# A planned attention and MLP kernel: weight loads on a second queue, more key and query buffers, a step split in two, and a new order

## The chip, the cores and the metric

The kernel runs on one core of a Trainium2 chip. Its engines are TensorE (PE in the profile, with its weight loads as PEld), VectorE (DVE), ScalarE (ACT), GpSimd (POOL) and SyncE (SP). SP, ACT and POOL each have a queue from which they issue transfers (DMAs). The metric is the device time of one execution in microseconds (us), as the median of several runs.

## The reference

Eight batches and eight heads of head dimension 64 are computed. There are 512 local and 32 global positions in a batch. A local query attends to all 32 global keys and to the local keys within 32 positions of it; a global query attends to all 544 keys. The attention output, 4352 tokens of width 512, goes through an MLP.

```python
s_g   = scale * q_g @ concat(k_g, k_l).T;   out_g = softmax(s_g) @ concat(v_g, v_l)
s_ll  = where(|i - j| <= 32, scale * q_l @ k_l.T, -1e9)
s_lg  = scale * q_l @ k_g.T
out_l = softmax(concat(s_lg, s_ll)) @ concat(v_g, v_l)
x     = concat(out_g, out_l) as tokens x 512
out   = gelu(x @ w_in) @ w_out              # w_in 512 x 2048, w_out 2048 x 512
```

All is float32.

## The kernel before

**Units and chunks.** Attention is cut into 64 units: a batch, a half of its sequence (256 queries) and a pair of heads. Four units make one chunk, the 256 tokens of a batch's half, which then goes through the MLP; 16 such chunks and one for all global tokens ("g") make 17 passes of the MLP. A unit's steps are: its loads (lk, lq, lv), transposes of keys and queries (tk, tq), copies of these to SBUF (k1, q1), scores (s, L408, and sg for the global queries, L565), mask and maximum (m, L427), the exponential (e, on ACT), the scaling (n, then nf and ns), transposes of the attention weights (t, L482 to L485), copies of these (ah), the product with the values (o, L519 or L532), and copies to the MLP's input (x). In a chunk's MLP, h is the first product (L707, or L711 to L713), g the GELU, mo the second product (L738, or L746 to L748), ob the copy of the result and ow its store.

**Precision.** The first eight units and the first chunk's MLP use plain float32 products. Later ones use pairs of a high and a low part, three products instead of one.

**Weights.** There are 32 loads of 512 KB (wl, L152 and L156), 16 of w_in and 16 of w_out. Each is worked on by w1 (L161 on DVE or L163 on ACT), w2 (L167, ACT) and w3 (L172, DVE) before the first chunk's MLP uses it, and by w4 and w5 (high and low part) before the second chunk's does. The raw loads have 16 buffers. Load number i also waits for w1 of load i - NW, with NW = 10. All 32 loads are issued from SP's queue.

**Loads of the first eight units.** They come in pairs of units. Keys go out on SP's queue, the first two pairs' queries on ACT's and the others' on SP's, and values on POOL's queue, nine transfers for a pair. The float32 keys and queries of a unit are copied into tiles of tag k1 and q1 with the unit's parity, so that two units have a place each.

**The order.** Nothing is ordered by hand. A planner in the kernel file gives each step a cost (DUR), a due time (from formulas, and OFF by kind of step), engines that may do it (EARLY, LATER), what it needs, and which buffers it takes and frees. It then plays a list schedule, and the instructions are emitted in the order of that play; each engine runs its own in that order. For transfers the planner keeps one running time of the DMA engines.

**The scaling.** st_n (L451 to L461) adds a small constant to the sums, takes the reciprocal, and multiplies 128 x 512 weights by it, all on DVE. nf (L468) and ns (L473) then write scaled copies of the edges; t waits for ns.

**The end.** The last chunk's two results (ob, t = 0 and 1) are copied from PSUM, each by one instruction. For "g" each is stored by four transfers: for t = 0 all four on SP's queue, for t = 1 two on SP's and two on ACT's.

## Time and profile before

| what | value |
|---|---|
| time, median of 3 runs | 1037.21 us (1036.88 to 1037.89) |
| the profiled execution's own time | 1037.63 us |
| its span, first to last instruction | 1035.8 us |
| PE busy | 1011.0 us (98%) |
| PEld busy | 898.3 us (87%) |
| DVE busy | 660.2 us (64%) |
| ACT busy | 688.2 us (66%) |
| POOL busy | 400.1 us (39%) |
| mean granted TensorE clock | 0.999 |
| moved by DMA | 72.29 MB, mean 70 GB/s |

Busy time is the time in which an engine has an instruction of its own under way; waits for semaphores and the issuing of DMAs from SP and ACT are not in it. Matmuls are pipelined, and their ends are modelled. The time of an execution stands 1.8 us above its span, which is what lies around the program.

### The profile page before, as it was taken

The page shows a single profiled execution, that of the slowest core. Times are in us where ns is not written, and L with a number is a line of the kernel's source. Part 1 is how long each engine was busy: PE and PEld are TensorE (multiplying, and loading weights), DVE is VectorE, ACT ScalarE, POOL GpSimd, SP SyncE. Part 2 cuts the span into 40 slices and gives each one's busy share as a digit, 9 for nine tenths or more (in the row PEclk, how much of TensorE's full clock was granted, in tenths as well). Part 3 has the DMA queues.
Part 4 walks back from the last instruction along what each step waited for, and adds up shares of the span by engine and source line. Part 5 has one row for each costly group of instructions (what it writes and reads, how often), then busy time and mean ns, then how long its engine had stood idle before and what let it go on. Part 6 is the DMA issues. An engine that isn't in the chain of part 4 may idle for free.

```text
span 1035.8 us, 21369 instructions
## 1 busy us (share of the span) xinstructions
PE 1011.0 (98%) x7000; PEld 898.3 (87%) x7000; DVE 660.2 (64%) x2068; ACT 688.2 (66%) x1637; POOL 400.1 (39%) x462
## 2 busy tenths in 40 slices
PE   7989999999999999999999999999999999999998
PEld 4656688899998999999998999999998999999997
DVE  3889757677676857677776667676776677651000
ACT  4889865777676866776677756676777757663231
POOL 6322676424333334243343434243343434233121
PEclk9999999999999999999999999999999999999999
DMA  6995222223323223222322323222322323210000
GB/s 148 279 316 149 51 68 47 49 63 60 71 40 73 41 61 60 58 50 54 65 51 60 66 61 61 59 48 55 71 45 62 62 61 62 49 28 22 22 21 21
DMA packets 271519, 72.29 MB, mean 70 GB/s; under 512 B 255984, under 2 KB 264432, under 8 KB 271408
## 3 DMA queue, kind: packets, MB, share of 16 engines
q1 hardware_dynamic: 267920, 68.44, 28.9%
q0 software_dynamic: 1280, 1.84, 0.7%
q8 instruction: 55, 0.90, 0.4%
q10 hardware_dynamic: 2208, 0.66, 0.3%
q14 instruction: 56, 0.46, 0.2%
HBM read 61.41 MB, written 9.44 MB: 68 GB/s over the span
## 4 chain that ended last, share of the span: by engine, by line
PE 88%; DVE 4%; DMA 3%; ACT 3%; issue 1%; SPq 1%; DVEq 0%; ACTq 0%
PE h L711 12%; PE acc L746 11%; PE h L712 11%; PE h L713 11%; PE acc L748 11%; PE acc L747 11%; PE o L519 5%; PE s L408 4%; DMA wraw<-in_moe_w_in_dram 3%; PE t L482 2%; PE go L652 2%; PE sg L565 1%; PE t L483 1%; PE acc L738 1%; ACT a_t L281 1%
## 5 line engine op out<-in xcount | busy, mean ns | idle before, releaser
L141 POOL TENSOR_TENSOR gl<-gf,gh 128x512 fp32r<-128x512 f32 x127 | 166.0, 1307 | 353.7 <-ACT gh L134 257.8
L711 PE MATMUL h<-xh,wh 128*128 128x256 f32 x1024 | 294.2, 287 | 0.0
L712 PE MATMUL h<-xl,wh 128*128 128x256 f32 x1024 | 286.3, 280 | 0.5 <-DVE xl L141 0.5
L713 PE MATMUL h<-xh,wl 128*128 128x256 f32 x1024 | 285.9, 279 | 0.0
L746 PE MATMUL acc<-wh,gh 128*128 128x512 f32 x512 | 205.9, 402 | 0.0
L748 PE MATMUL acc<-wl,gh 128*128 128x512 f32 x512 | 200.7, 392 | 0.0
L747 PE MATMUL acc<-wh,gl 128*128 128x512 f32 x512 | 200.3, 391 | 0.0
L711 PEld LDWEIGHTS h<-xh,wh 128*128 128x128 f32 x1024 | 192.7, 188 | 7.7 <-ACT gf L281 0.6
L712 PEld LDWEIGHTS h<-xl,wh 128*128 128x128 f32 x1024 | 192.7, 188 | 5.9 <-DVE xl L141 0.7
L713 PEld LDWEIGHTS h<-xh,wl 128*128 128x128 f32 x1024 | 194.1, 190 | 0.0
L281 ACT ACTIVATE gf<-h 128x512 f32<-128x512 f32 x136 | 81.2, 598 | 80.9 <-PE h L713 48.9
L281 ACT ACTIVATE a_t<-a_t,sm 128x192 f32<-128x192 f32 (+1 forms) x256 | 116.6, 457 | 4.5 <-DVE sm L433 3.9
L748 PEld LDWEIGHTS acc<-wl,gh 128*128 128x128 f32 x512 | 96.1, 188 | 21.3
L141 POOL TENSOR_TENSOR vs<-vr,vs 128x512 fp32r<-128x512 f32 x56 | 73.0, 1303 | 98.2 <-ACT vs L134 39.2
L746 PEld LDWEIGHTS acc<-wh,gh 128*128 128x128 f32 x512 | 96.3, 188 | 12.8
L134 ACT ACTIVATE gh<-gf 128x512 fp32r<-128x512 f32 x106 | 67.0, 632 | 60.4 <-PE acc L748 58.2
L747 PEld LDWEIGHTS acc<-wh,gl 128*128 128x128 f32 x512 | 96.5, 188 | 11.6 <-POOL gl L141 0.3
L502 DVE TENSOR_TENSOR at<-t,at 128x512 fp32r<-128x512 f32 x112 | 68.5, 617 | 49.9 <-ACT at L134 49.3
L427 DVE CUSTOM_DVE_ANT_0 a_t<-s,mask 128x192 f32<-128x192 f32 (+1 forms) x256 | 78.9, 367 | 25.4 <-PE s L408 25.4
L281 ACT ACT_TABLE_LOAD x67 | 86.0, 1283 | 1.1
L134 ACT ACTIVATE at<-t 128x512 fp32r<-128x512 f32 x112 | 60.0, 543 | 31.8 <-PE t L483 16.1
L545 ACT ACTIVATE xs<-o 64x256 f32<-64x256 f32 x112 | 42.6, 381 | 52.3 <-PE o L519 49.5
(140 smaller groups left out, 1743.0 us busy)
## 6 DMA issues: line engine op xcount, KB each, us to landing
wraw<-in_moe_w_in_dram SPq DMA_DIRECT2D x16, 512.0 KB, 7.5
raws<-in_v_l_dram SPq DMA_DIRECT2D x64, 128.0 KB, 2.5
wraw<-in_moe_w_out_dram SPq DMA_DIRECT2D x16, 512.0 KB, 9.0
out_dram<-ob SPq DMA_DIRECT2D x32, 256.0 KB, 2.3
raws<-in_k_l_dram SPq DMA_DIRECT2D x224, 36.0 KB, 1.9
raws<-in_q_l_dram SPq DMA_DIRECT2D x224, 32.0 KB, 1.8
vr<-in_v_l_dram SPq DMA_DIRECT2D x112, 64.0 KB, 2.2
raws<-in_v_g_dram SPq DMA_DIRECT2D x128, 16.0 KB, 2.0
```

Source lines behind the costliest of these rows:

```text
L134: nc.scalar.activation(out=out, in_=in_, func=AF.Copy)
L141: (nc.vector if e == "v" else nc.gpsimd).tensor_sub(**kw)
L281: nc.scalar.activation(func=func, **kw)
L427: nc.vector.tensor_tensor_reduce(out=a_t[:, j, aoff[half][i]:aoff[half][i] + w], in0=s[:, c:c + w], in1=masks[half][i], scale=1.0, scalar= ...
L502: nc.vector.tensor_sub(out=at[:, 1], in0=st.pop((u, "t", j))[:, :n * P].rearrange("p (n q) -> p n q", q=P), in1=at.bitcast(F32)[:, 0])
L519: nc.tensor.matmul(out=o[:, :, qsl], lhsT=l.rearrange("p s e -> p (s e)"), rhs=r, start=(n == 0), stop=(n == 3), skip_group_check=True)
L711: nc.tensor.matmul(out=h, lhsT=hi, rhs=xh, start=(c == 0 and not (key == (0, 0) and f < HQ and f % 2)), stop=False, skip_group_check=True)
L712: nc.tensor.matmul(out=h, lhsT=hi, rhs=xl, start=False, stop=False, skip_group_check=True)
L713: nc.tensor.matmul(out=h, lhsT=lo, rhs=xh, start=False, stop=(c == NCC - 1), skip_group_check=True)
L746: nc.tensor.matmul(out=acc[t], lhsT=gh[:, f % 2, tsl], rhs=hi, start=(f == 0), stop=False)
L747: nc.tensor.matmul(out=acc[t], lhsT=gl[:, f % 2, tsl], rhs=hi, start=False, stop=False)
L748: nc.tensor.matmul(out=acc[t], lhsT=gh[:, f % 2, tsl], rhs=lo, start=False, stop=(f == NF - 1))
```

## The change

- A weight's load may be issued from SP's or from POOL's queue; of the 32, 24 now go out on POOL's. The load waits for w1 of the load 12 places before it, not 10. Values of the first eight units may go out on SP's queue or POOL's.
- The float32 keys and queries of the first eight units have four places instead of two (tags k1, k2 and q1, q2, each with the unit's parity).
- The big multiplication leaves st_n and becomes a step st_nm of its own. For the first eight units the planner may put it on POOL or DVE, later on DVE. nf needs n only; t needs nm and ns.
- The last result (t = 1 of "g") is copied in two halves, one by ACT and one by DVE. For t = 0 of "g" two of the four stores move from SP's queue to POOL's.
- The second pair's queries' load waits for the transposes of the first unit's keys; tq of a unit comes after its tk; the first weight's load comes after lh of batch 0 instead of lk of the first unit.
- The planner's costs, its due times (OFF, and a new table TWEAK by step) and its model of transfers change: it now counts eight transfers in flight for POOL's queue and eight for the others together. With this the order of the whole program is new.

```diff
-    "n": 1.08, "nf": {"p": 1.0, "v": 0.36}, "ns": {"p": 0.42, "v": 0.22}, "t0": 0.44, "t1": 0.33,
+    "n": 0.24, "nm": {"v": 0.8, "p": 1.25}, "nf": {"p": 0.65, "v": 0.36}, "ns": {"p": 0.42, "v": 0.22}, "t0": 0.44, "t1": 0.33,
...
-NW = 10
+NW = 12
...
-            (nc.sync if e == "s" else nc.scalar).dma_start(out=raw, in_=w_out.bitcast(I32)[f * P:(f + 1) * P, :])
+            (nc.sync if e == "s" else nc.gpsimd).dma_start(out=raw, in_=w_out.bitcast(I32)[f * P:(f + 1) * P, :])
...
-        t = ap_.tile([P, CH], F32, name="qt", tag=f"q1{u[2] % 2}")
+        t = ap_.tile([P, CH], F32, name="qt", tag=f"q{1 + second(u)}{u[2] % 2}")
...
-        t = ap_.tile([P, NB, 32], F32, name="kt", tag=f"k1{u[2] % 2}")
+        t = ap_.tile([P, NB, 32], F32, name="kt", tag=f"k{1 + second(u)}{u[2] % 2}")
...
+    def st_nm(e, u):
+        a_t = a_ts[u[2] % 2]
...
-        nc.vector.tensor_tensor(out=av, in0=av, in1=edges(u)[0].unsqueeze(3).to_broadcast([P, 2, 2, P]), op=ALU.mult)
+        (nc.vector if e == "v" else nc.gpsimd).tensor_tensor(out=av, in0=av, in1=edges(u)[0].unsqueeze(3).to_broadcast([P, 2, 2, P]), op=ALU.mult)
...
-        copy(e, o, acc)
+        if key == "g" and t:
+            copy("a", o[:, 0:CH], acc[:, 0:CH])
+            copy("v", o[:, CH:DM], acc[:, CH:DM])
+        else:
+            copy(e, o, acc)
...
-                (nc.sync if t == 0 or n % 2 == 0 else nc.scalar).dma_start(out=out[r0:r0 + SG, :], in_=o[32 * n:32 * n + 32])
+                ((nc.sync, nc.gpsimd)[n % 2] if t == 0 else (nc.sync, nc.scalar)[n % 2]).dma_start(out=out[r0:r0 + SG, :], in_=o[32 * n:32 * n + 32])
...
-        step(("wl", n), w_load, (n,), "s", due - 6.0, [("w1", wl[i - NW])] if i >= NW else [], [("wr", n)], issues=0.9, size=0.36, after=("wl", wl[i - 1]) if i else ("lk", units[0]))
+        step(("wl", n), w_load, (n,), "sp", due - 6.0, [("w1", wl[i - NW])] if i >= NW else [], [("wr", n)], issues=1, size=0.36, after=("wl", wl[i - 1]) if i else ("lh", 0))
...
-        if k in "as" and x["size"]:
-            t = max(t, dma - (1.5 if k == "a" else 2.7))
+        if x["size"] and len(lanes[k == "p"]) > 7:
+            t = max(t, lanes[k == "p"][-8] + 0.1)
```

## Rows read from the trace of the kernel before

**Rows 1.** Windows: busy time (count) by engine, granted clock, DMA share, GB/s.

```profile
4.24:25.00 20.76, 17.70 (x70) 11.52 (x70) 8.97 (x37) 9.06 (x30) 12.50 (x24) 1.00 0.70 147
25.00:110.00 85.00, 76.22 (x415) 54.76 (x415) 73.17 (x211) 74.54 (x163) 29.41 (x40) 1.00 0.78 234
110.00:200.00 90.00, 86.30 (x568) 72.03 (x567) 66.33 (x181) 66.06 (x160) 55.80 (x53) 1.00 0.26 52
200.00:1030.80 830.80, 830.42 (x5954) 759.99 (x5953) 511.74 (x1642) 536.68 (x1283) 298.76 (x330) 1.00 0.25 52
```

**Rows 2.** Waits of PE over the span: total us, times, longest.

```profile
PE sg L565 <- DMA vrb<-in_v_g_dram: 2.3, 1, 2.3
...
PE kp L321 <- ACT kt L134: 1.3, 2, 0.7
...
PE kp L321 <- ACT qt L134: 1.0, 2, 0.6
```

**Rows 3.** Timeline of ACT, first 30 us; idle before and releaser in brackets.

```profile
17.38 0.38 ACT L134 ACTIVATE qt<-qp 128x256 f32<-128x256 f32 x1 [1.67 <-PE s L408]
...
26.09 0.38 ACT L134 ACTIVATE qt<-qp 128x256 f32<-128x256 f32 x1 [0.24 <-PE s L408]
```

**Rows 4.** Timeline of PE, first 30 us.

```profile
9.00 1.86 PE L408 MATMUL s<-kt,qt 64*128 64x192 f32 x8
...
24.98 0.97 PE L408 MATMUL s<-kt,qt 64*128 64x192 f32 x8
```

**Rows 5.** Timeline of SP's queue: its first issue and its first weights' issue.

```profile
0.76 0.45 SPq L304 DMA_DIRECT2D raws<-in_k_l_dram  x1
...
23.01 1.69 SPq L152 DMA_DIRECT2D wraw<-in_moe_w_in_dram  x3
```

**Rows 6.** The raw weights' tile, to 110 us: durations in ns, first and last start.

```profile
L172 DVE SCALAR_TENSOR_TENSOR wf<-wraw x32: 673/684/1943, 31.9 to 100.1; 128x512 int32<-128x512 int32 x32
L161 DVE TENSOR_SCALAR wraw<-wraw x18: 412/428/2027, 28.9 to 95.0; 128x512 int32<-128x512 int32 x18
...
DMA to landing us min/median/max: 3.9/8.4/14.4
```

**Rows 7.** Timeline of POOL: issues of value loads at three times, and a subtraction.

```profile
5.08 1.68 POOL L253 DMA_DIRECT2D vr<-in_v_l_dram  x2
...
30.24 1.53 POOL L253 DMA_DIRECT2D vr<-in_v_l_dram  x2 [13.30 <-PE o L532]
...
57.38 0.54 POOL L264 DMA_DIRECT2D vrb<-in_v_g_dram  x1 [2.17 <-DMA vrb<-in_v_l_dram]
57.93 1.56 POOL L141 TENSOR_TENSOR vgs<-raws,vgs 128x640 fp32r<-128x640 f32 x1
```

**Rows 8.** Timeline of DVE beside the second issue and the subtraction.

```profile
30.80 0.69 DVE L461 TENSOR_TENSOR a_t<-a_t,sm 128x512 f32<-128x512 f32 x1
...
58.11 2.03 DVE L161 TENSOR_SCALAR wraw<-wraw 128x512 int32<-128x512 int32 x1
```

**Rows 9.** Groups of DVE and POOL to 110 us: busy us, mean ns, idle before.

```profile
L461 DVE TENSOR_TENSOR a_t<-a_t,sm 128x512 f32<-128x512 f32 x8 | 5.5, 692 | 0.3
...
L468 POOL TENSOR_TENSOR ge<-a_t,sm 128x256 f32<-128x256 f32 x2 | 1.2, 612 | 20.3 <-PE t L483 20.3
```

**Rows 10.** The values' tile vrb, loaded from POOL: issue to landing, to 110 us.

```profile
DMA to landing us min/median/max: 2.8/4.8/7.3
```

**Rows 11.** Timelines of SP and ACT at the end.

```profile
1030.51 2.73 SPq L761 DMA_DIRECT2D out_dram<-ob  x6
...
1031.24 0.60 ACT L134 ACTIVATE ob<-acc 128x512 f32<-128x512 f32 x1 [0.76 <-PE acc L748]
```

**Rows 12.** Timeline of PE in the middle, after a transpose.

```profile
507.42 0.37 PE L711 MATMUL h<-xh,wh 128*128 128x256 f32 x1
507.62 0.28 PE L712 MATMUL h<-xl,wh 128*128 128x256 f32 x1
507.74 0.28 PE L713 MATMUL h<-xh,wl 128*128 128x256 f32 x1
```

More of the change, by code (lines that the diff above doesn't have):

```diff
@@ L778, in step @@
         nodes[name] = dict(name=name, fn=fn, args=args, due=due, needs=[x for x in needs if x is not None], after=after,
-                           takes=list(takes), frees=list(frees), size=size, table=table, port=port and name[0] in PORT,
+                           takes=list(takes), frees=list(frees), nd=issues, size=size, table=table, port=port and name[0] in PORT,
                            eng=({k: d[k] for k in eng} if isinstance(d, dict) else
-                                {k: (d if not issues else 0.57 * issues) for k in eng}))
+                                {k: (d if not issues else 0.53 * issues) for k in eng}))
     wl = [0, 2, 4]
@@ L820, in attn_mlp @@
                 step(("lk", u), load_kn, (u,), "s", s0 - 15.0, [], [("kn%d" % second(u), u)], issues=5 + half, size=0.33, after=("lk", units[n - 2]) if n else None)
[L821 removed]
+                step(("lq", u), load_qn, (u,), "a" if n < 4 else "s", s0 - 14.0, [("tk", units[0])] if n == 2 else [], [("qn%d" % second(u), u)], issues=2, size=0.26, after=("lq", units[n - 2]) if n else None)
             step(("tk", u), st_tkn, (u,), "t", s0 - 5.0, [("lk", pair)] + pv(("tq",)), [("h", (u, "k"))], [("kn%d" % second(u), pair), ("kgr", b)], dur="tkn")
[L823 removed]
+            step(("tq", u), st_tqn, (u,), "t", s0 - 3.5, [("lq", pair), ("tk", u) if n else None], [("h", (u, "q"))], [("qn%d" % second(u), pair)], dur="tqn")
             kb, qb = [("h", (u, "k"))], [("h", (u, "q"))]
@@ L867, in attn_mlp @@
         if n < NPE and not odd:
-            step(("lv", u), load_v, (u, 2), "p", f0 - 18.0, [], [("vs", (u, "r"))] if second(u) else [("vr0", u), ("vr1", units[n + 1])], issues=9, size=0.5, after=("lv", units[n - 2]) if n else None)
+            step(("lv", u), load_v, (u, 2), "sp", f0 - 18.0, [], [("vs", (u, "r"))] if second(u) else [("vr0", u), ("vr1", units[n + 1])], issues=9, size=0.5, after=("lv", units[n - 2]) if n else None)
             step(("vm", u), st_vm, (u, 2), "p", f0 - 8.0, [("lv", u)])
@@ L950, in attn_mlp @@
         for t in range(2):
-            step(("ob", key, t), ml_e, (key, t), "va" if key == "g" and t else "a", C0 + W * (NF + LAG) + 1.5 + 0.1 * t,
+            step(("ob", key, t), ml_e, (key, t), "a", C0 + W * (NF + LAG) + 1.5 + 0.1 * t,
                  [("mo", key, NF - 2 + t if key == "g" else NF - 1), ("ob", key, 0) if t and key != "g" else None], [("at%d" % (1 - t), (key, t, "o"))], [("acc", key)])
@@ L978, in attn_mlp @@
             x["due"] += off[0 if c == 0 else 1 if c == 1 else 2 if c < 4 else 3]
+    classes = {}
+    for i, x in enumerate(nodes.values()):
+        x["due"] += TWEAK.get(i, 0.0)
+        nm = x["name"]
+        if len(nm) > 1 and isinstance(nm[1], tuple) and 2 * nm[1][0] + nm[1][1] > 3:
+            x["due"] += TWEAK.get(-1 - classes.setdefault((nm[0], *nm[1][1:], *nm[2:]), len(classes)), 0.0)
     left = {}
@@ L997, in attn_mlp @@
     dma = port = 0.0
+    lanes = {False: [], True: []}
     table = "exp"
@@ L1065, in attn_mlp @@
         if x["size"]:
-            dma = max(dma, t + 0.5) + x["size"] / 0.26
-            end = max(end + 2.2, dma + 0.8)
+            busy[k] = t
+            for i in range(x["nd"]):
+                lane = lanes[k == "p"]
+                busy[k] = max(busy[k], lane[-8] + 0.1 if len(lane) > 7 else 0.0) + (0.64 if k == "p" else 0.53)
+                dma = max(dma, busy[k]) + x["size"] / x["nd"] / 0.26
+                lane.append(dma + 1.9)
+            end = dma + 1.9
         got[x["name"]] = end + (0.16 if k == "t" else 0.0)
```

45 lines of the change are left out of this document (24 added, 21 removed), and 160 rows, old and new, of tables (DUR, OFF, TWEAK).

## The prediction, made before the changed kernel ran

> **What bounds the kernel now.** I read the windows first, since the page's 98% for PE is an average over stages that differ. From 200 us to PE's last product PE is busy 830.42 of 830.80 us [rows 1]: nothing but the number and pace of its own products counts there. From 110 to 200 us it is idle 3.70 us, from 25 to 110 us 8.78 us, and from 4.24 to 25 us 3.06 us [rows 1]. Since PE takes everything in one order, the end moves by what these gaps lose or win, by the pace of the first stretch, and by the tail behind the last product. The change can win only there.
>
> The first stretch has a second loss. Eight score products take 1.86 us at 9 us and 0.97 us at 25 us [rows 4], though the granted clock reads 1.00 throughout [rows 1]: until then TensorE goes at half pace, the lower of its levels (1.2 against 2.4 GHz), after a stretch with short gaps. 17.70 us of PE's time lie there [rows 1].
>
> Next come PE's waits. They are short and spread: the longest after 25 us is 2.3 us before one sg, and the transposes of keys wait 2.3 us in four places for ACT's copies of keys and queries [rows 2]. Then I asked why those copies are late. ACT stood for 1.67 and 0.24 us before two copies of queries until PE had done the scores of an earlier unit [rows 3]. That is the place being held by the unit two before, the thing of which there are two.
>
> Last come the weights. SP issues from 0.76 us, and its first weight goes out at 23.01 us [rows 5], behind 38 other transfers by the timeline, 0.58 us each. The first w1 starts at 28.9 us and the last w3 at 100.1 us [rows 6]. From 25 to 110 us DVE is busy 73.17 and ACT 74.54 of 85 us [rows 1]; both carry the weights' steps beside the attention of eight units. In the stretch before, DVE is busy 8.97 of 20.76 us, and the DMA engines 0.70 of it [rows 1].
>
> **The change part by part.**
>
> *Four places for keys and queries.* It removes waits like those of ACT in [rows 3]. Of the 2.3 us that PE lost behind such copies [rows 2] nothing excludes that all goes, and nothing that a copy is then late for another reason (ACT's other work), so from 0 to -2.3. I take half, -1.2, since one of the two waits that I can name ended after 0.24 us only.
>
> *24 weights on POOL's queue.* The cost of an issue on POOL is 0.54 to 0.84 us by the value loads (0.54 for one, 1.68 for two [rows 7]), so 24 take 13 to 20 us of POOL. POOL is busy 29.41 of 85 us in the long stretch and stood for 13.30 us before 30.24 us [rows 1, 7]; the issues fit beside it, and in the order of play some wait. What it wins: weights can go out before 23 us. The DMA engines have 30% of 20.76 us free there, 6.2 us. In the long stretch they move 234 GB/s at a share of 0.78 [rows 1], so 300 GB/s when full, and one weight of 524 KB takes 1.75 us: 3.5 weights come forward. Each costs DVE 0.428 us in 18 of 32 cases and 0.684 us always [rows 6], 0.925 us on average, so 3.2 us of DVE's work leaves the full stretch for an emptier one. Of PE's 8.78 idle us there I take 3.2 as won by it; the bounds are 0 (PE's waits there are not for weights by name) and all 8.78.
>
> *The eight-in-flight count.* At 57.38 us POOL waited 2.17 us with an issue for an earlier load to land. Behind it stood a subtraction of 1.56 us [rows 7]. Beside that, DVE's w1 took 2.03 us where the median is 0.428 [rows 6, 8], and then the sg that waited 2.3 us on PE came [rows 2]. The planner now counts such waits and can order round them. From 0 to -2.3; I take half, -1.2, since the weights' loads bring new ones.
>
> *Scaling as its own step.* It was 8 x 0.692 = 5.5 us of DVE in the first 110 us [rows 9]. On POOL, half the elements take 0.612 us [rows 9], so 1.22 us each. If all eight moved, DVE would win 5.5 us; but [rows 7, 8] show a DVE instruction held for 1.6 us beside a POOL one, and then each could cost DVE 1.22 - 0.69 = 0.53 us more, 4.2 in all. I take 0, between the two, for PE. Later units keep all of it on DVE, where DVE is busy 511.74 of 830.80 us [rows 1]: covered by PE; without that cover one more small start per unit.
>
> *Load order.* The second pair's query load goes behind the first unit's key transposes, and tq behind tk. Queries of the first unit are not held. I cost it at 0: until 25 us PE has gaps that take it; if it is late, what is late next is the third unit's tq, 1 us at the half pace.
>
> *110 to 200 us.* The waits there hang on ACT's and DVE's copies of the second chunk, which stay. 0; bounds -3.7 (all idle time) and +1.0 (a quarter more).
>
> *The new order, later.* PE's time there is set by its own sequence. After a transpose the first product takes 0.20 us until the next one starts, and the others 0.12 [rows 12]. 64 units with two groups of transposes, each followed by a product, pay 64 x 2 x 0.08 = 10 us now if none stand together. A new order may pair or part some: I take 0, and a tenth, 1.0 us, to either side.
>
> *The tail.* Six stores go out on SP's queue in 2.73 us, 0.455 each, from 1030.51 us; the last copy runs from 1031.24 for 0.60 us [rows 11]. SP's two stores for t = 1 can thus start at 1032.33, not at 1031.84. With two on SP and two on POOL, SP is free at 1031.42, the half copies end between 1031.54 and 1031.84 (half of 0.60, or all), and SP's last store goes out 0.5 to 0.8 us earlier. POOL's two issues end by 1031.6 at 0.54 each [rows 7], and land 2.8 to 7.3 us behind issue by [rows 10], the low end without traffic beside them; that is 1033.9 to 1038.4, where SP's sixth is issued by 1033.24. So from -0.8 to +3; I take -0.4, near the low end, because no other transfer is under way.
>
> **Sum.** -1.2 - 3.2 - 1.2 + 0 + 0 - 0.4 = -6.0 us. The profiled execution's 1037.63 us (1035.8 of span and 1.8 around it) becomes 1031.6; it stands 0.4 us above the median, so from 1037.21 the forecast is 1031.2 us.
>
> **The Trainium skill.** Two issues on POOL took 1.68 us at 5.08, and 1.53 us at 30.24, where DVE had its two-input multiplication beside them, which itself took its usual 0.69 us [rows 7 to 9]. [...] And "DMA: Bandwidth & Descriptors", section "Issuing engines are not separate DMA queues", says that issuing from several engines saves only issue time, which is the second rival's mechanism.
>
> **Rivals.**
>
> *More than forecast.* All gaps from 4.24 to 110 us that I named go: 2.3 + 8.78 = 11.1, so 1026. For it: DVE and ACT stand at 86 to 88% there [rows 1], so there is room. Against: PE's waits are on many different things.
>
> *No change.* The transfers share the same DMA engines, which from 25 to 110 us are busy 0.78 of the time [rows 1]; a weight that comes earlier pushes back keys, queries or values, and PE waits for those. The tail alone is left: 1036.8. For it: 8.4 us from issue to landing of a weight [rows 6], a queue that is already deep. Against: the free 30% before 25 us.
>
> *Slower: POOL as a queue with waits in it.* POOL does all in order. A weight's issue that waits there, for w1 of the load 12 before or for one of eight to land, holds nm, nf, ns and the value loads behind it, and then t and PE. [rows 7, 8, 2] show one such case: 2.17 us on POOL, 2.3 us on PE. At 2.3 us each, 2.6 more cases eat the 6.0 us, and from 3.5 on the kernel is slower beyond what can be told; five give 1037.2 - 6.0 + 11.5 = 1042.7. For it: 20 of 32 loads lie beyond the first 12. Against: POOL is two thirds idle there.
>
> *Slower: issues held by DVE.* If each of 24 issues waits out a DVE instruction of 0.692 us [rows 9], POOL loses 16.6 us; on the path, 1037.2 - 6.0 + 16.6 = 1047.8. The issues of [rows 7] speak against it. [...]
>
> **How the numbers follow.** Forecast, a gain of 2.1 to 9 us: 0.57. More: 0.10. No change: 0.16. POOL's waits: 0.15. Held issues: 0.02. What a measurement of this kernel can tell from no change is about 0.2%, 2.1 us. So faster 0.67, same 0.16, slower 0.17. The range goes from 1025.0 (a gain of 12, where the larger gain's case ends) to 1040.0; beyond it are some 0.05 below and 0.13 above. The likeliest case alone spans 1028 to 1035.
>
> **What would show it.** Right: the first w1 well before 28.9 us and the last w3 some 3 to 6 us before 100.1; PE's idle time from 25 to 110 us near 4.4 us; no ACT wait on PE's scores before a query copy; PE busy without gap from 200 us, with the same length for that stretch; the last store some 0.5 us nearer to PE's end. Wrong: POOL waiting on DMA or w1 while PE waits at t; POOL issues above 1 us; weights that land no earlier; or a middle that is longer by more than 1 us, since there the whole argument has no term.

## The result and the profile after

The changed kernel takes 1044.32 us (median of 6 runs, 1040.67 to 1046.73), the kernel before beside it 1037.24. The ratio is 1.0064, with a 95% interval of 1.0042 to 1.0086: slower by 4.4 to 8.9 us, where 6.0 us of gain had been forecast, and outside the forecast's range. A second set of 5 runs (e15, below) gave 1041.63 us and a ratio of 1.0054 (1.0040 to 1.0069). The profiled execution took 1040.67 us, the fastest of the first set: what its rows show is the least that the change costs.

First the windows, as in [rows 1]: length, then busy time and count for PE, PEld, DVE, ACT and POOL, granted clock, DMA share and GB/s.

```profile
4.24:25.00 20.76, 15.46 (x54) 9.11 (x54) 9.87 (x37) 8.16 (x26) 15.95 (x28) 1.00 1.02 258
25.00:110.00 85.00, 76.94 (x401) 55.52 (x400) 69.45 (x192) 70.07 (x162) 35.77 (x50) 1.00 0.70 205
110.00:200.00 90.00, 89.91 (x627) 77.77 (x626) 72.84 (x206) 65.95 (x152) 46.73 (x47) 1.00 0.28 54
200.00:1030.80 830.80, 826.56 (x5915) 751.68 (x5914) 531.78 (x1657) 527.17 (x1264) 310.26 (x343) 1.00 0.25 52
```

Length less PE's busy time is PE's idle time. Against [rows 1] it goes from 3.06 to 5.30 us in the first stretch, from 8.78 to 8.06 in the second, from 3.70 to 0.09 in the third, and from 0.38 to 4.24 in the last. That is +2.2, -0.7, -3.6 and +3.9, in sum +1.8; PE's last product starts at 1032.58 us instead of 1030.82. Behind it stand 6.2 us to the span's end instead of 5.0. So the span goes from 1035.8 to 1038.8 us, and the sum closes. A gain in the third stretch is eaten by losses in the first, the last and the end.

The first stretch. The weights come early, as forecast. This is the raw weights' tile to 110 us, answering [rows 6]: median duration in ns between least and most, first and last start.

```profile
L303 DVE SCALAR_TENSOR_TENSOR wf<-wraw x32: 670/684/693, 21.2 to 92.3; 128x512 int32<-128x512 int32 x32
L292 DVE TENSOR_SCALAR wraw<-wraw x21: 408/422/1439, 17.1 to 87.1; 128x512 int32<-128x512 int32 x21
L283 POOL DMA_DIRECT2D wraw<-in_moe_w_in_dram x12: 748/753/915, 5.1 to 70.4; - x12
...
DMA to landing us min/median/max: 4.5/9.4/21.0
```

The first weight goes out at 5.1 us instead of 23.01 [rows 5], twelve more from 12.99 to 23.62 us; the first w1 starts at 17.1 us instead of 28.9, the last w3 at 92.3 instead of 100.1, and no weight's issue on POOL takes over 0.92 us. But the landings of these thirteen lengthen one after the other, from 4.6 to 12.1 us (the 21.0 us belong to a later weight, issued by SP at 62.20 us). And what shares the DMA engines with them comes late. The timeline at 30 us:

```profile
29.50 0.31 DVE L498 STREAM_TRANSPOSE qg<-qg 128x128 f32<-128x128 f32 x1 [6.20 <-DMA qg<-in_q_g_dram]
29.74 0.65 DVE L267 COPY ao<-t 128x512 f32<-128x512 f32 x1
...
30.49 0.87 PE L666 MATMUL o<-ao,vr 128*64 128x128 f32 x3 [5.21 <-issue]
```

DVE stands for 6.20 us until the second batch's global queries land, 16 KB each. Behind that transpose stands the copy ao of the first unit, and PE stands 5.21 us for it. The name "issue" says only that PE's sequencer waited; the row of DVE tells for what.

The half pace of the first stretch lasts longer too, though the granted clock reads 1.00 in all these windows. In the kernel before, the score products were at full pace at 24.98 us [rows 4]. Here two sg products take 1.33 us before the stand, all 16 products o behind it still go at half pace, and full pace is there at 33.71 us (timeline of PE):

```profile
20.55 1.33 PE L699 MATMUL sg<-kt,gs 128*128 128x288 f32 x2 [0.60 <-DVE sm L558]
...
30.49 3.29 PE L666 MATMUL o<-ao,vr 128*64 128x128 f32 x16 [5.21 <-issue]
33.71 0.75 PE L699 MATMUL sg<-kt,gs 128*128 128x288 f32 x2
```

The row of 3.29 us has all 16 products, the one of 0.87 us above the first three. In e3, below, the same 16 take 1.96 us, from 23.98 us.

The last stretch. Waits of PE from 200 us on (total us, times, longest), in the kernel before:

```profile
PE gx L668 <- DVE gos L663: 0.4, 1, 0.4
```

The same in the changed kernel:

```profile
PE o L653 <- DVE at L636: 3.1, 4, 0.9
PE t L616 <- DVE xs L685: 0.5, 1, 0.5
```

A copy by DVE of the transposed weights (at, low part) is late four times, three of them 117 us apart, the length of a batch (two chunks). The timeline at the first of these:

```profile
453.90 1.28 POOL L272 TENSOR_TENSOR gl<-gf,gh 128x512 fp32r<-128x512 f32 x1 [6.26 <-ACT gh L265]
454.07 1.29 DVE L267 CAST k<-kt 128x320 fp32r<-128x320 f32 x1
...
456.61 0.55 DVE L636 TENSOR_TENSOR at<-t,at 128x384 fp32r<-128x384 f32 x1
...
457.22 0.50 PE L653 MATMUL o<-at,vs 128*128 128x256 f32 x2 [0.88 <-DVE at L636]
```

The copy of a key block took 1.29 us here, where the kernel before has a mean of 0.324 us for it. It started 0.17 us behind a subtraction of POOL and ended 0.18 us after that one did. The at that PE needs stands behind it on DVE.

The end, answering [rows 11]:

```profile
1032.27 2.54 SPq L899 DMA_DIRECT2D out_dram<-ob  x4
1032.54 1.06 POOL L899 DMA_DIRECT2D out_dram<-ob  x2 [8.39 <-ACT ob L265]
1033.01 0.38 ACT L265 ACTIVATE ob<-acc 128x256 f32<-128x256 f32 x1 [0.76 <-PE acc L882]
1033.42 0.42 DVE L267 COPY ob<-acc 128x256 f32<-128x256 f32 x1 [3.75 <-ACT ob L265]
1033.88 0.94 ACTq L899 DMA_DIRECT2D out_dram<-ob  x2
```

The two halves run one behind the other: DVE's waits for ACT's. Together they take 0.83 us, where one copy took 0.60.

### The profile page after: what moved, and what is told of

It is laid out like the page before. It is cut to its first block, busy times and chain, and to the rows that moved or that the text cites. A ratio compares the mean times of both kernels' runs of the same rounds, so it can differ in the third digit from the quotient of the medians.

```text
span 1038.8 us, 21384 instructions
## 1 busy us (share of the span) xinstructions
PE 1011.5 (97%) x7000; PEld 895.7 (86%) x7000; DVE 684.4 (66%) x2092; ACT 673.6 (65%) x1606; POOL 413.4 (40%) x485
## 4 chain that ended last, share of the span: by engine, by line
PE 81%; DVE 5%; ACT 5%; DMA 4%; SPq 2%; issue 2%; POOL 1%; DVEq 0%; ACTq 0%; POOLq 0%
PE h L845 10%; PE h L846 10%; PE h L847 10%; PE acc L880 10%; PE acc L882 10%; PE acc L881 10%; PE o L653 5%; PE s L539 4%; PE t L616 2%; PE h L841 2%; PE acc L872 2%; ACT a_t L412 2%; PE go L786 2%; DMA raws<-in_k_l_dram 1%; PE sg L699 1%
## 5 line engine op out<-in xcount | busy, mean ns | idle before, releaser
L845 PE MATMUL h<-xh,wh 128*128 128x256 f32 x1024 | 297.3, 290 | 0.0
L636 DVE TENSOR_TENSOR at<-t,at 128x512 fp32r<-128x512 f32 (+1 forms) x112 | 68.4, 616 | 28.1 <-ACT at L265 27.0
L684 DVE TENSOR_TENSOR xs<-o,xs 64x256 f32<-64x256 f32 x112 | 46.3, 413 | 60.0 <-ACT xs L679 58.8
L653 PE MATMUL o<-at,vs 128*128 128x256 f32 x448 | 72.8, 284 | 3.2 <-DVE at L636 3.1
```

The lines of the kernel that those rows point to most:

```text
L636: nc.vector.tensor_sub(out=at[:, 1], in0=st.pop((u, "t", j))[:, :n * P].rearrange("p (n q) -> p n q", q=P), in1=at.bitcast(F32)[:, 0])
L653: nc.tensor.matmul(out=o[:, :, qsl], lhsT=l.rearrange("p s e -> p (s e)"), rhs=r, start=(n == 0), stop=(n == 3), skip_group_check=True)
L845: nc.tensor.matmul(out=h, lhsT=hi, rhs=xh, start=(c == 0 and not (key == (0, 0) and f < HQ and f % 2)), stop=False, skip_group_check=True)
```

## The experiments

Three numbers tell the kernels apart; they stand in the table at the end of this section. "Work at 200 us" counts every product of PE that has started by then at the usual interval of its shape, taken from the trace of before (in all 897.7 us); it doesn't depend on the order. Where an order is mixed, the planner's play is replaced by a written list of steps and engines:

```diff
-    while any(ready.values()):
...
+    for name, on in PLAY:
+        nodes[name]["on"] = on
+        order.append((0.0, len(order), nodes[name]))
```

**e1 and e2: the two halves of the order.** Joined at planned time 200 us.

> All steps that the changed kernel's planner starts before 200 us stand as in the changed kernel, all others in the order, and on the engines, of the kernel before. Theory 'later order': the changed kernel is 4 us ahead in PE's work at 200 us and loses it and more afterwards to its new order; then this run gives about 1037.2 - 4 = 1033 us, and its runs lie within 1 or 2 us of each other as those of before do. Rival 'start': the loss is made in the first 60 us, where transfers crowd; then this run stays at the changed kernel's 1041 to 1046 us.

> The opposite cut: steps that the planner of before starts before 200 us stand as before (weights on SP's queue), all others in the new order. 'Later order': 1037.2 + 5 to 10 us, 1042 to 1047, with the wide spread of the changed kernel. 'Start': 1037 us.

Measured: e1 1044.51 us, ratio 1.0068 (1.0053 to 1.0083); e2 1046.91 us, 1.0085 (1.0067 to 1.0104). Both joins cost time of their own, so the times decide nothing: e1 has waits of 1.56, 1.20 and 2.82 us between 213 and 221 us, and a granted clock of 0.5 for 3.4 us behind them. But the traces speak. From 300 us on e1 has the pace of the kernel before and 0.4 us of waits; e2 has waits on the same copy as the changed kernel, 3.6 us in four. The waits belong to the later order.

**e3: the weights back on SP's queue.**

```diff
-            (nc.sync if e == "s" else nc.gpsimd).dma_start(
+            nc.sync.dma_start(
```

> The changed kernel in its own order, but each weight's load issued from SP's queue at the same place of the order. If the POOL queue is what brings weights forward without holding others, this run is slower than the changed kernel by some 5 us (weights behind the other issues again, as far as SP gets). If the weights of the POOL queue crowd the first units' small loads, the 5.2 us wait of PE at 25 us shrinks and the run is faster than the changed kernel by 3 to 6 us.

Measured: 1038.66 us, ratio 1.0011 (1.0001 to 1.0020). So POOL's queue costs the changed kernel 0.43 to 0.53%, 4.5 to 5.5 us, where a gain of 3.2 was forecast. The stand of 5.2 us is gone. The list of transfers to 40 us (count, KB, median us to landing) shows why; the changed kernel first, then e3.

```profile
wraw<-in_moe_w_in_dram POOLq DMA_DIRECT2D x8, 512.0 KB, 8.4
...
raws<-in_k_l_dram SPq DMA_DIRECT2D x5, 32.0 KB, 10.4
...
qg<-in_q_g_dram SPq DMA_DIRECT2D x8, 16.0 KB, 5.2
```

```profile
wraw<-in_moe_w_in_dram SPq DMA_DIRECT2D x8, 512.0 KB, 6.6
...
raws<-in_k_l_dram SPq DMA_DIRECT2D x5, 32.0 KB, 2.3
...
qg<-in_q_g_dram SPq DMA_DIRECT2D x8, 16.0 KB, 1.8
```

The same 13 weights are issued by 40 us in both; by then all 13 have landed in the changed kernel and 8 in e3. In one queue they stand behind the small loads that are wanted first; from a second queue they run beside them, and a 32 KB load takes 10.4 us instead of 2.3. Most of the stand is made up later in the profiled executions: at 200 us the changed kernel is 0.7 us of work behind e3 (table).

**e4: the load that PE stood for, moved.** The steps that load and transpose the second batch's global queries come 25 and 40 us later in the written list; nothing else is moved.

```diff
-('lh', 1) and ('tg', 1) at their planned times
+('lh', 1) 25 us later, ('tg', 1) 40 us later
```

> The changed kernel, but the load of batch 1's global queries and its transpose on DVE stand 25 and 40 us later in the order. Theory: PE's wait of 5.2 us before the first unit's product with the values came from DVE, which stood 6.2 us for that load, crowded by twelve weights, with the copy of the attention weights behind it. Then the wait goes, TensorE leaves the half pace earlier, and the time falls by 5 to 8 us. Rival: the first unit's values themselves land late; then PE still waits there, and the time stays within 2 us.

Measured: 1043.36 us, 1.0061 (1.0046 to 1.0076): no gain. The stand went from this load to the keys (6.8 us at 36.3), with a clock of 0.5 for 10.2 us from 32.5. It is the crowd, not one load.

**e5: new order at the start, old order later, weights on SP.** As e3, joined at 400 us, where the two orders have done like steps.

> The changed kernel, with all weights' loads issued by SP, and from planned time 400 us on with the order and the engines of the kernel before. Theory (two losses: the GpSimd queue at the start, some 5.7 us, and the new order of the later steps, some 4 to 5 us; the new order of the first 200 us is a gain): at 200 us PE is 4.7 us of work ahead of the kernel before, as in e3, and keeps it; PE's gaps from 450 us on are under 0.5 us; time 1037.4 - 4.7 + 1.2 (the end with the two halves) = 1034, between 1032.5 and 1035.5. Rival (the later order costs nothing, e3's loss behind 200 us lies in the weights or the end): as e3, 1038 to 1039.5. Second rival (a join costs more than it saves, as in e1): waits of PE of 3 us and more between 400 and 430 us, and 1037 or more.

Measured: 1033.25 us, ratio 0.9967 (0.9954 to 0.9979), as the theory had it; e18, the same kernel again, gave 1034.21 and 0.9963 (0.9949 to 0.9976). Against e3 the old later order is worth 0.44%, 4.6 us. One wait of 0.5 us, at 342 us, is left behind 200 us; e3 has 3.4 us in five. Such a wait costs more than its row says: at 457 us in the changed kernel 1.27 us pass from the start of one product to that of the next, where 0.23 is usual, for a row of 0.88. This kernel beats both.

**e6: POOL's queue alone, in the old order.**

```diff
+        q = nc.sync if n in (11, 16, 19, 24, 21, 26, 23, 28) else nc.gpsimd
...
-            (nc.sync if e == "s" else nc.scalar).dma_start(
+            q.dma_start(
```

> The kernel before, its order kept, with the 24 weights' loads that the change moves issued from GpSimd's queue and nothing else changed. Theory (the weights' transfers, no longer held back by SP's queue, take the DMA engines from the small loads that the first products wait for): the first weight is issued before 10 us instead of at 23.0 us, the DMA share of 5 to 30 us rises, PE stands longer before its first products than in the kernel before, and the time is 2 to 6 us above it, 1039.5 to 1043.5. Rival (the prediction: weights' arithmetic starts earlier and feeds PE, SP's queue is free for keys and values): 1028.4 to 1037, with PE's idle time between 25 and 110 us shorter. Second rival (the queue only hurts in the new order of the start): within 1 us of the kernel before.

Measured: 1039.38 us, 1.0020 (1.0010 to 1.0030), some 2 us slower. The first weight goes out at 17.0 us, not before 10, and the first w1 runs at 28.5, hardly earlier than before (28.9): an earlier load alone brings no earlier arithmetic, since DVE does its steps in their old order.

**e7: four places alone; e8: the end alone.** e7 changes only the tags; e8 only the halved copy and two stores, as in the change.

```diff
-        t = ap_.tile([P, CH], F32, name="qt", tag=f"q1{u[2] % 2}")
+        t = ap_.tile([P, CH], F32, name="qt", tag=f"q{1 + second(u)}{u[2] % 2}")
```

> The kernel before, its order kept, with four places each for the float32 keys and queries, and nothing else changed. The prediction put this part at -1.2 us, between 0 and -2.3 (PE's waits for the buffers kt and qt at the first products). Theory: PE's waits at the first transposes for kt shrink, and what comes next (loads, the copies) takes part of it: 1035 to 1037.4. Rival (the place was the last to come only by name, the loads come as late): no change, 1037.0 to 1037.8, with waits of the same length on another releaser.

> The kernel before, with the end of the changed kernel alone: the last output tile copied in two halves by ACT and DVE, and the stores of the first tile on SP and GpSimd, those of the last on SP and ACT. Theory (both halves are written into one tile, and the second waits for the first; a store of GpSimd takes 0.3 us longer to issue): the DVE half starts behind the ACT half, PE's last product to the span's end is 6.0 to 6.3 us instead of 5.0, and the time 1 us above the kernel before, 1038 to 1038.8. Rival (the prediction): -0.4 us, 1036.6 to 1037.4, with the two halves side by side. Second rival (the loss at the end of the changed kernel came from what else ran there): halves one behind the other, but the end no later than before.

Measured: e7 1036.55 us, 0.9999 (0.9990 to 1.0008); e8 1037.29 us, 1.0002 (0.9993 to 1.0011). In e7 PE waits for the copies of keys and queries as long as in [rows 2]:

```profile
PE kp L321 <- ACT kt L134: 1.3, 2, 0.7
PE kp L321 <- ACT qt L134: 0.9, 2, 0.5
```

ACT no longer stands for PE's scores before a copy of queries, as forecast, but PE's waits stay. In e8 the halves run one behind the other, and the end is still only 5.1 us: SP's last store is issued 0.3 us earlier, ACT's 0.3 us later, and the last landing comes 0.1 us later than before.

**e9, e12 and e19: what holds the later order.** All are e3 with one more change. e9 and e12 let ACT copy a key block that the new order gives to DVE; e9 that of unit (0, 3), e12 that of unit (0, 0), which is the one in the rows above. e19 leaves all engines and changes DVE's order at four places: the late at goes ahead of the key copy, its subtraction and the scaling of the global scores. In the written lists, for e12 and for e19:

```diff
-(('k1', (4, 0, 0)), 'v')
+(('k1', (4, 0, 0)), 'a')
```

```diff
+(('al', (3, 1, 2), 1), 'v')
 (('k1', (4, 0, 0)), 'v')
 (('k2', (4, 0, 0)), 'v')
 (('gn', (3, 1)), 'v')
-(('al', (3, 1, 2), 1), 'v')
```

> As e3 (the changed kernel, weights' loads all from SP), with one thing changed: in the last four batches the copy of the keys of unit (0, 3) of a batch, which the new order puts on DVE, runs on ACT, in the same place of the order. In the changed kernel this copy is the one that took 1.29 us instead of 0.33 beside GpSimd's 1.28 us subtraction, and the copy that PE's products then waited 0.88 us for stood behind it. Theory (the loss of the later order is DVE copies that fall beside GpSimd's subtractions): the three waits of 0.87 us, at 457, 574 and 691 us, shrink to under 0.2 us, and the time is 2 to 3 us under e3's 1038.7, 1035.7 to 1036.7. Rival (the order leaves too little slack there, whatever runs long): the waits stay, on this or another releaser, and the time is 1038 to 1039.5.

> As e3 (the changed kernel, weights' loads all from SP), with one thing changed: the copy of the keys of unit (0, 0) of the last four batches runs on ACT instead of DVE, in the same place of the order. This is the copy that takes 1.29 us beside GpSimd's subtraction while the copy that PE's products wait for (0.87 us) stands behind it; e9 moved the copy of another unit and left this one on DVE. Theory (DVE copies that fall beside GpSimd's subtractions): the waits of PE of 0.87 to 0.9 us, one in each batch, shrink to under 0.2 us; time 2 to 3.5 us under e3's 1038.7, 1035.2 to 1036.7. Rival (no slack in the new order, whatever runs long): the waits stay, on this or another releaser; 1038 to 1040.

> As e3 (the changed kernel, weights' loads all from SP), with four changes in DVE's order alone, one in each of batches 3 to 6: the low part of the second transposed block of unit (1, 2), which PE's products wait for, is put ahead of the next batch's key copy, its subtraction and the scaling of the global scores, three instructions that stood before it and of which one falls beside GpSimd's subtraction. Every instruction stays on its engine; the other engines' orders don't change. Theory (a held DVE instruction costs only because PE's next products stand behind it; e12 moved the hold from the key copy to the scaling behind it, 1.16 us instead of 0.50, and won 2.4 us): the waits of PE on this copy near 457, 574, 691 and 808 us are gone, each two chunks take some 115.4 us instead of 117.1, and the time is 3.5 to 5.5 us under e3's 1038.7: 1033.2 to 1035.2. Rival (the copy itself is held beside GpSimd's subtraction then, or the keys that are late now are waited for): waits of 0.5 us and more remain on it or on the keys, 1036 or more.

Measured: e9 1042.52 us, 1.0046 (1.0033 to 1.0060); e12 1036.21 us, 0.9998 (0.9988 to 1.0007); e19 1037.17 us, 1.0001 (0.9992 to 1.0010). e9 was the wrong copy: the held one stayed on DVE, and four new waits of 0.5 us on a low part of at came, 25 us behind each of the old ones. e12's median lies where its theory had it, 2.4 us under e3's; by the ratios, which set each kernel against the one before on its own chip, it won 1.3 us, and e19 1.0, a fifth to a third of what its theory said; the intervals leave some 1.4 us to either side, so neither gain is clear of noise. (All differences below are by the ratios.) The timeline of e12 at the same place tells what is left:

```profile
451.82 1.61 POOL L395 TENSOR_TENSOR gl<-gf,gh 128x512 fp32r<-128x512 f32 x1 [6.47 <-ACT gh L388]
...
452.57 1.16 DVE L857 TENSOR_SCALAR sgr<-sgr,gsm 128x544 f32<-128x544 f32 x1
...
453.65 0.54 DVE L759 TENSOR_TENSOR at<-t,at 128x384 fp32r<-128x384 f32 x1
```

With the key copy gone, the scaling of the global scores, 0.50 us elsewhere, is the one held beside POOL, 0.66 us too long where the key copy had been 0.97. In e19 the at is in time, and what DVE does later is late instead (waits of PE from 200 us on):

```profile
PE t L739 <- DVE xs L808: 2.0, 6, 0.5
```

So the traces show both the hold and the want of slack; the times alone don't. Two chunks (192 of the split products of the MLP's second half) take 115.6 us in the kernel before and in e5; in the new order 117.1 with the held copy, 116.4 to 116.6 in e12 and e19 (117.4 once, with a wait near 712 us), and 115.3 where no wait falls in. Which batches have it differs between executions of the same kernel: the changed kernel had a wait of 0.9 us at 457, 574 and 691 us in one profile, and at 808 us too in the other.

**e10 and e13: the early weights held back.** e10 lets a weight go on POOL's queue only when the one four places before has passed w3, e13 holds twelve of them until the second pair's keys have landed.

```diff
+        if n == 2:
+            nc.gpsimd.tensor_copy(out=hold, in_=kns[0][:, 9, 0:1])
```

> The changed kernel with its weights' loads on GpSimd's queue as they are, but held to four ahead: from the fifth on, GpSimd first copies one element of a column of the weight four places earlier as it leaves its last step, so the load can't start before that. The order is the changed kernel's, except that a load stands behind the step that it now waits for. Theory (twelve weights of 512 KB at once crowd the small loads): the 32 KB loads of the second pair's keys land in under 5 us instead of 10.4, PE's stand of 5.2 us at 25 to 30 us is gone or under 2 us, and the time falls from 1044.3 to 1038.5 to 1041.5. Rival (GpSimd's queue costs by itself, by its issuing or by weights' arithmetic that runs earlier): 1043 to 1046 with the stand still there. Second rival (what stands behind a held load in GpSimd's queue is late in its turn): the stand goes, another of GpSimd's steps (values' loads, the edges' scaling) is what PE waits for between 40 and 80 us, and 1042 or more.

> The changed kernel with its weights' loads on GpSimd's queue as they are, but for one hold: ahead of the second weight GpSimd copies one column of the second pair's keys, so eleven early loads start when these keys have landed, near 23 us instead of 12.99. Nothing else differs, except that a clearing of values' edges stands ahead of the hold. Theory (the crowd: twelve weights of 512 KB delay the small loads issued beside them): the global queries of the second batch land some 2 us behind their issue, DVE doesn't stand for them, PE's stand of 5 us at 25 to 30 us is gone or under 2 us, and the time is 1038 to 1041, as e3's, with 1.1 us for the longer end. Rival (GpSimd's queue costs by itself): 1043 to 1046. Second rival (the crowd is only moved, to the keys of the next pair and GpSimd's own values): PE stands 3 us and more between 30 and 60 us, 1041.5 or more.

Measured: e10 1083.32 us, 1.0440 (1.0416 to 1.0464); e13 1044.50 us, 1.0070 (1.0057 to 1.0083). e10 is its second rival at a far higher price: each hold stops all that stands behind it on POOL, and the weights come so late that PE stands 10.8 and 9.0 us for steps on DVE. The granted clock is 0.5 for 51 us in all between 40 and 140 us there, which is part of the price. In e13 the stand at 25 to 30 us is gone, PE stands 4.8 us at 80 us instead, and the crowd has moved on, as its second rival had it, only later. Transfers from 24 to 52 us, first in e3 and then in e13:

```profile
raws<-in_q_l_dram SPq DMA_DIRECT2D x2, 128.0 KB, 8.5
rawb<-in_q_l_dram SPq DMA_DIRECT2D x2, 128.0 KB, 8.5
...
kgr<-in_k_g_dram SPq DMA_DIRECT2D x4, 16.0 KB, 5.4
```

```profile
raws<-in_q_l_dram SPq DMA_DIRECT2D x2, 128.0 KB, 13.6
rawb<-in_q_l_dram SPq DMA_DIRECT2D x2, 128.0 KB, 22.8
...
kgr<-in_k_g_dram SPq DMA_DIRECT2D x4, 16.0 KB, 11.8
```

**e11 and e16: the end, and the queue without its bytes.** e11 is the changed kernel with the first tile's four stores back on SP. e16 is e3 with a load of 512 bytes on POOL's queue wherever the changed kernel has a weight there; nothing reads what it loads.

```diff
-                ((nc.sync, nc.gpsimd)[n % 2] if t == 0 else (nc.sync, nc.scalar)[n % 2]).dma_start(out=out[r0:r0 + SG, :], in_=o[32 * n:32 * n + 32])
+                (nc.sync if t == 0 or n % 2 == 0 else nc.scalar).dma_start(out=out[r0:r0 + SG, :], in_=o[32 * n:32 * n + 32])
```

```diff
+        if e == "p":
+            nc.gpsimd.dma_start(out=tiny[:, n % 8:n % 8 + 1], in_=w_out.bitcast(I32)[0:P, n:n + 1])
```

> The changed kernel with the four stores of the first of the last two output tiles back on SP, none on GpSimd; the halved copy stays. Theory (a queue of GpSimd that has carried the weights ends later: the last product to the span's end was 6.2 us in the three profiles that have both the weights and stores on it, and 5.0 to 5.3 in the others): 5.0 to 5.3 us, and 1043.2, 1.1 under the changed kernel's 1044.3. Rival (the 1.1 us come from the weights on that queue, whether it stores or not): 6.2 us, 1044.3. Its start is the changed kernel's, so it is a second look at that: stand of PE near 25 to 30 us of some 5 us, and where the granted clock falls behind it, for 3 to 10 us, the time lies above the 1040.7 of the changed kernel's profiled execution.

> As e3 (the changed kernel, weights' loads all from SP), and at the 24 places of GpSimd's queue where the changed kernel issues a weight, GpSimd issues a load of 4 bytes a partition, 512 bytes in all, into a tile that nothing reads. Theory (the bytes of the weights, which SP's order held back, crowd the small loads; the queue costs nothing by itself): as e3, 1037.5 to 1039.5; PE has done as much work at 200 us as in e3. Rival (GpSimd's queue, its issuing and its turn among the queues, costs by itself): 2 us and more above e3, 1040.7 to 1044.5. For the end: if the 6.2 us from the last product to the span's end come from the number of loads on GpSimd's queue, they are here too, and if from the weights' bytes, 5.0 to 5.3 as in e3.

Measured: e11 1040.82 us, 1.0042 (1.0025 to 1.0059), with 4.9 us behind the last product; e16 1041.20 us, 1.0043 (1.0026 to 1.0059), with 6.2 us. The end of 6.2 us is in all seven profiles that have both 24 more transfers on POOL's queue and stores on it (the changed kernel twice, e1, e4, e10, e13, e16), and in none of the others, among them e6 and e17 with the weights alone and e3, e5 and e8 with the stores alone. What ends late is not a landing: the last store lands 3.9 us behind the start of the last product in the changed kernel and 3.8 in e3. It is a DRAIN, an instruction of POOL's own queue, the longest of the three with which that queue closes (the changed kernel, then e3; durations in ns, least, median and most):

```profile
L1286 POOLq DRAIN  x3: 46/102/5027, 1033.0 to 1038.5; - x3
```

```profile
L1316 POOLq DRAIN  x3: 46/102/3768, 1031.6 to 1036.1; - x3
```

Without stores on POOL the long DRAIN starts 9.8 us before the last product and is hidden, though it takes 4.35, 5.57 and 6.31 us with 36, 51 and 60 transfers on that queue in the program (before, e11, e6). With stores it starts 0.4 us behind the start of the last product and takes 3.3 to 3.9 us with 29 or 38 transfers, and 5.0 with 53, e16's tiny ones included. So the number of transfers counts, not their bytes; why a DRAIN takes longer behind more of them isn't shown. At the start e16 lost nothing (table): there it is the bytes. But it was 3.3 us slower than e3, as its rival had it; 1.1 of it is the end, and in the profiles the rest lies in two more waits of the later order (61.2 and 59.4 us for chunks that took 59.5 and 57.7 in e3). The wait on the held copy comes three or four times in every profile of the new later order with these transfers on POOL's queue (the changed kernel twice, e4, e10, e11, e13, e16) and in e2, e3 and e9 without them. The other wait, near 716 us, is in three of those seven (0.53 to 1.37 us) and not in e2 or e3. Whether the queue brings that one or chance does is not settled.

**e15, e17 and e18: the changed kernel again, and the start alone.** e17 is e5 with the changed kernel's weights on POOL and the old stores.

> The changed kernel itself, for a second profile and more runs beside the others of this set. Theory (its spread, 1040.7 to 1046.7, comes from whether the granted clock falls behind PE's stand at 25 to 30 us): the stand is there again, the median is 1042.5 to 1045, and an execution over 1042 shows a stretch of 3 to 10 us at clock 0.5 before 110 us, one of 1041 or less none. Rival (the spread comes from elsewhere): no such stretch in a slow execution.

> As e5 (the changed order to planned time 400 us, then the order before), but with the changed kernel's 24 weights on GpSimd's queue, and the four stores of the first of the last two tiles on SP as before. The later order has no waits here, and the end none of GpSimd's stores, so what is left between this and e5 is the start alone. Theory (at the start GpSimd's queue costs what the traces show at 200 us, 0.6 to 1.4 us of work; the rest of what it cost the changed kernel came later, from the 1.1 us at the end and from waits of the later order): 1033.7 to 1035.2, and 4.9 to 5.2 us from the last product to the span's end. Rival (the queue costs its 3 to 5 us at the start, in most executions more than the profiled ones show): 1036 to 1038.5.

> e5 once more, beside the run above and on its chip: 1032.5 to 1034.5 again, and so faster than the kernel before by 0.2 to 0.45%. Rival (the first result leaned on its six executions): 1035 or more.

Measured: e15 1041.63 us (1041.50 to 1043.92); e17 1035.44 us (1033.86 to 1040.61), 0.9984 (0.9972 to 0.9996). e15's profiled execution, at 1041.53, has the stand (4.8 us) and no recorded fall of the clock, so the executions above 1042 us stay unexplained by a profile. The mean granted clock of each execution doesn't settle it: it is 0.999 in the three fastest of the changed kernel's eleven and 0.994 to 0.998 in the others, but 0.998 in the slowest, and e11's fastest has 0.996. e17 falls between its theory and its rival: 0.21% behind e18, 2.2 us. In the windows of its profile the granted clock shows a fall (0.5 from 28.2 us, for 6.8 us) beside the stand; full pace comes at some 35 us, where the changed kernel has it at 33.7 without a recorded fall:

```profile
25.00:60.00 35.00, 27.50 (x161) 20.95 (x161) 25.98 (x79) 22.21 (x59) 13.56 (x24) 0.90 0.86 231
```

| kernel | work at 200 us | last product | to the span's end | median us | ratio |
|---|---|---|---|---|---|
| before | 122.7 | 1030.8 | 5.0 | 1037.2 | |
| changed | 126.7 | 1032.6 | 6.2 | 1044.3 | 1.0064 |
| changed again (e15) | 126.8 | 1033.4 | 6.2 | 1041.6 | 1.0054 |
| e3, weights on SP | 127.4 | 1031.2 | 5.1 | 1038.7 | 1.0011 |
| e16, 24 tiny loads on POOL | 127.8 | 1033.0 | 6.2 | 1041.2 | 1.0043 |
| e12, key copy on ACT | 128.2 | 1029.3 | 5.1 | 1036.2 | 0.9998 |
| e19, DVE's order | 127.3 | 1029.9 | 5.1 | 1037.2 | 1.0001 |
| e5, old order later | 126.9 | 1026.4 | 5.2 | 1033.3 | 0.9967 |
| e17, e5 with POOL's weights | 125.2 | 1028.6 | 4.9 | 1035.4 | 0.9984 |
| e6, before with POOL's weights | 119.6 | 1033.8 | 5.0 | 1039.4 | 1.0020 |

## Why the prediction was wrong

*24 weights on POOL's queue, -3.2: the wrong sign.* This is the largest failure. The step that failed is that PE wins what DVE is relieved of, because the DMA time before 25 us is free to be filled. The weights did come earlier, w1 at 17.1 us, and DVE's busy time from 25 to 110 us fell by 3.7 us, near the 3.2 forecast. But PE's idle time there fell by 0.7 us only, and before 25 us it rose by 2.2: the 6.2 us of DMA time that were free there were what kept the small loads quick. The longer half pace comes on top; the prediction names this pace as a loss of its own, but no part of the change has a term for it. Measured, the queue costs 4.5 to 5.5 us (e3 against the changed kernel): some 2.2 at the start (e17 against e18; the work at 200 us in the table gives 0.6 to 1.7), 1.1 at the end, and 1 to 2 that aren't placed. By e16 the crowd of bytes is the smaller part: 3.3 us of the cost, with 2 us to either side, stay when only tiny loads stand on the queue. The rival "no change" had the mechanism, an earlier weight that pushes back keys and queries, but no price: it let the push only cancel the gain. By the Trainium skill, "DMA: Bandwidth & Descriptors", section "Issuing engines are not separate DMA queues", transfers of all engines interleave on the same 16 DMA engines; the landings above, 2.3 to 10.4 us, agree.

*The new order, later, 0 with 1.0 to either side: mis-sized.* It costs 4.6 us (e5 against e3). The prediction looked for its range in the pairing of transposes and products, and that is nearly the same: in the profiles from 300 to 1000 us 119 switches from a transpose to another product, 124 before. By the traces the cost lies where no term stood, in a DVE instruction that is held beside POOL's subtraction with a copy for PE queued behind it; no kernel that takes away one hold or its effect won it back in time (e12, e19). [rows 8] had shown just such a hold, 2.03 us for a step of 0.43, and the prediction used it only for the first 110 us. The Trainium skill, "SBUF — State Buffer", section "SBUF: two separate sides", has DVE and GpSimd share a port pair that one of them keeps for its whole instruction; the key copy that ended 0.18 us behind the subtraction agrees.

*Four places, -1.2.* 0 (e7: -1.0 to +0.8 us). ACT's wait for a place went, but PE's waits behind the copies stayed, 2.2 us after 2.3: the copies were late for other reasons, as the smaller bound had it. In the rival *More than forecast* one of these waits, 0.57 us at 26.52 us, is counted twice, since it lies within the 8.78; all gaps come to 10.5 us, not 11.1. The forecast doesn't hang on it.

*110 to 200 us, 0, and the eight-in-flight count, -1.2.* Too small together. PE's idle time from 110 to 200 us fell from 3.70 to 0.09 us, the prediction's bound for it. With all weights on SP the new order of the first 200 us does 4.2 to 5.5 us more of PE's work by then than the old (e3, e5, e12, e18 against 122.7), and e5 turns it into 3.4 us of time. What in that order brings it wasn't taken apart; the scaling as its own step and the load order are in it.

*The tail, -0.4.* Alone 0.2 us (e8: -0.7 to +1.1). With the weights on POOL's queue +1.1 to 1.2, at a place where the prediction had a bound of +3 for another reason, a late landing: POOL's stores landed 2.0 us after their issue, and its DRAIN was late. The two halves, in one tile, ran one behind the other, 0.83 us for both.

*The rivals on the slower side.* POOL's issues were not held by DVE (0.98 us at most, for a load of values), so that rival falls. That POOL holds its steps behind waiting issues is what e10 does at its worst; in the changed kernel POOL's waits for DVE and for landings before issues are there, 1.4 us at most before 25 us, but PE's stand hung on DVE.

The changed kernel's 4.4 to 8.9 us are thus -3.4 to -3.8 for the start's order, +4.6 for the later order and +4.5 to 5.5 for POOL's queue, in sum +5.3 to 6.7. The sum closes nearly by construction, since each kernel is set against the next, and the intervals leave 1.6 to 2.5 us to either side of the last two. Open are why POOL's DRAIN grows with the transfers on its queue, what the 1 to 2 us are that aren't placed, why the first set of runs reached 1046.7 us where the second stayed under 1044, and whether the wait near 716 us comes with POOL's queue.

## What to carry to other kernels

Here a second queue filled the DMA engines earlier (a share of 1.02 instead of 0.70 before 25 us) and took away the order that one queue gave. So before moving bulk loads to a second queue, ask which small loads were quick only because the bulk stood behind them. An order that is full at every place pays for each instruction that runs long: look for DVE instructions that can fall beside POOL's with something for PE queued behind, and give such copies a place ahead. When one change holds several parts, join the old and new order at a place where both have done like work; here one part of the change, the start's order, was worth 3.4 us and the rest hid it.

## What the runs showed of the hardware that had not been expected

- The recorded granted clock falls to 0.5 for 3.4 to 10.2 us (17.1 once, in e10), mostly beside a stand of PE at the start: in e4 from 32.5 us for 10.2, in e11 from 28.4 for 6.8, in e13 from 80.8 for 3.4. It also does with no stand over 1.5 us beside it (e13 from 36.5 for 3.4), and with the weights on SP (e5 from 40.1 for 6.8).
- The record doesn't hold all of the half pace: in the changed kernel it reads 1.00 up to 110 us, while the 16 products behind the stand take 3.29 us instead of e3's 1.96.
- The hold beside POOL works both ways. POOL's subtraction of 128 x 512 took 1.61 us instead of 1.28 at 451.82 us in e12, where a two-input subtraction of DVE (k, 0.48 us) had started 0.03 us before it.
- POOL's closing DRAIN is longer with more transfers on its queue, of 512 bytes or 512 KB: 3.8 us with 38 and 5.0 with 53 where stores stand before it, 4.35, 5.57 and 6.31 with 36, 51 and 60 where none do. With stores at the end it shows, though 24 of the transfers were issued in the first 75 us.
